# One second-product unit a turn, and Strassen's seven products for the last ten g tiles of a fused attention and feed-forward kernel

## The chip, the cores and the metric

The kernel runs on one core of a Trainium2 chip. The metric is the device time of one execution in microseconds, the median of three runs. The core has five engines with queues of their own: PE (matmuls; PEld is its weight load), DVE (vector), ACT (scalar), POOL (GpSimd) and SP, which issues most DMAs. [...]

## The reference

Cosine attention over 8 batches of 12 heads, 448 positions, 64 wide, and then a feed-forward layer with a hard swish:

```
q_n = q / (norm(q) + 1e-06);  k_n = k / (norm(k) + 1e-06)
scores = q_n @ k_n.T / tau
attn = exp(scores - max) ;  attn = attn / (sum + 1e-09)
x = (attn @ v), heads side by side         # 3584 tokens x 768
h = x @ w_in                               # 768 -> 2048
g = h * clip(h + 3, 0, 6) / 6
out = g @ w_out                            # 2048 -> 768, f32
```

## The kernel before

Heads are taken in pairs: 6 pairs a batch, 48 in all. A pair is a *turn* of the loop over `i`. The first 18 pairs run from an order written out by hand (`PLAN`); from `FIRST` = 18 on, the loop at the end of the kernel issues turn after turn, with every engine's order fixed by the program. Turn `i` issues on PE the rest of the values of pair i-1 (`VA`, L434), the scores of pair i (`SC`, L394) and a few *units* of the feed-forward layer for earlier batches, which fill PE while ACT does the exponentials (`EX`, L412). Batch b's feed-forward work lies in the turns of batch b+1 and later. After turn 47 there is no attention left, and units alone run to the end.

There are two kinds of unit, and each takes one PSUM bank from a ring of six (`bank_of(None)`). `mm1_unit(b, fc)` (L514, *first product*) multiplies 128 columns of `w_in` with the batch's x, transposed, in `xT`: six matmuls of 448 columns. ACT's relu (L523) and DVE's product (L529) turn it into a slab of `gT`. A batch has 16. `mm2_unit(b, t, m)` (L550, *second product*) multiplies a tile of 128 tokens of `gT` with a half (384 columns) of `w_out`: 16 matmuls. ACT (L561) or DVE (L563), in turns, copies the bank to an `o` tile, and SP stores it with two DMAs (L571). Two batches share a `gT` buffer of 7 tiles of 128 tokens, so that a batch with an even number has 3 tiles (6 units) and one with an odd number 4 (8 units).

`units[i]` says how many units turn i takes. Before, a batch's second-product units are spread with `n_lag`: one a turn, and two in the first and the last turn of a batch when 8 are to be placed. The first turn of a batch (i = 18, 24, 30, 36, 42) takes two first products that are left over and no new one; the new batch's first products begin in the turn after it. Each of those reads all six head pairs of the batch in `xT`. A pair's attention output reaches `xT` by a DMA transpose that SP issues: `back_two` (L498) for two pairs, `back_crossbar` (L486) for one. For the last pair of a batch it is issued in the first turn of the next, after `finish_values`, and in SP's queue behind what was queued earlier: the stores of `o`, the load of q or k (`load_qk`, L174) and, in every other turn, four loads of v (`load_v`, L186).

Other names that matter. `raws` are seven buffers of q or k as loaded (f32), `sqs` two of their squares, `vr` three of v. POOL squares (L203), normalises (`NM`, L246), casts v (L265) and copies a part of the keys (`km`, L351). DVE sums the squares (L215), copies keys (L341), finishes the values (L454, L455).

The two lines that place the second-product units of a batch:

```
n_lag = [len(lag) // 2 - 2, 1, 1, 1, 1, len(lag) // 2 - 2]
units[(b + 1) * HP + n] = carry + lag[: n_lag[n]] + u if n == 0 else carry + u + lag[: n_lag[n]]
```

After turn 47 come, in this order: two first products of batch 6, six second products of batch 6, the 16 first products of batch 7 and its 8 second products, the last one in two halves of 192 columns; one of the last half's two stores goes by ACT's queue.

Of the kernel before, what the change touches and what calls it, by code (L numbers as in the profile page):

```python
# [8 lines left out]
FP32 = mybir.dt.float32  # L9
BF16 = mybir.dt.bfloat16  # L10
AF = mybir.ActivationFunctionType
ALU = mybir.AluOpType
# [6 lines left out]
ORDER = "111111111111111111111111111111222222"  # L19
# [42 lines left out]
def kernel(  # L62
# [10 lines left out]
    nc = tc.nc  # L73
    B, H, S, D = q.shape
# [3 lines left out]
    HP = H // 2  # L78
    NP = B * HP
    CC = d_model // 128  # L80
    FCN = d_ff // 128
    MH = d_model // 2
# [8 lines left out]
    const = ctx.enter_context(tc.tile_pool(name="const", bufs=1))  # L91
# [20 lines left out]
    }  # L112
    at_n = {1: 0, 2: 0}
    NV, NR = 3, 7
    vr = [const.tile([128, 4, 5, D], FP32, name=f"vr{i}", tag=f"vr{i}") for i in range(NV)]
    NVX = 4
    vx = [const.tile([128, 8, D + 1], BF16, name=f"vx{i}", tag=f"vx{i}") for i in range(NVX)]
    raws = [const.tile([128, 2, 7, D], FP32, name=f"raw{i}", tag=f"raw{i}") for i in range(NR)]
    sqs = [const.tile([128, 2, 7, D], FP32, name=f"sq{i}", tag=f"sq{i}") for i in range(2)]
    nrms = [const.tile([128, 7, 2, D], BF16, name=f"nrm{i}", tag=f"nrm{i}") for i in range(3)]  # L120
    n2s = [const.tile([128, 2, 14], FP32, name=f"n2{i}", tag=f"n2{i}") for i in range(2)]
    rs = [
# [21 lines left out]
    def needs(*what):  # L144
        for w in what:
            assert w in issued or any(x < 0 for x in w[1:] if isinstance(x, int)), w
# [121 lines left out]
    unread = {}  # L268

    def bank_of(name, reads):  # L270

        bank = {"Y": Y, "Z": Z}[name] if name else next_bank()
        key = id(bank)
        assert not unread.get(key), name
        unread[key] = reads
        return bank, key
# [261 lines left out]

        post["a"].append(relu)

    def mm2_unit(b, t, m, end=None):
        assert not weights
        g = gT[(b // 2) % 2]
        ps, key = bank_of(None, 1)
        width = MH if end is None else MH // 2
        cols = slice(m * MH + width * (end or 0), m * MH + width * (end or 0) + width)
        for fc in range(FCN):
            c0 = (S + SR) * (b % 2) + 128 * t if t < 3 else SM
            lhs = g[:, fc, c0 : c0 + 128]
            nc.tensor.matmul(  # L550
                ps[:, 0:width],
                lhs,
                w_out_sb[:, fc, cols],
                start=(fc == 0),
                stop=(fc == FCN - 1),
            )

        def store():
            o = sb.tile([128, MH], FP32, name="o", tag="o", bufs=4)
            if on_act:  # L560
                nc.scalar.copy(out=o[:, 0:width], in_=ps[:, 0:width])  # L561
            else:
                nc.vector.tensor_copy(out=o[:, 0:width], in_=ps[:, 0:width])  # L563
            unread[key] = 0
            for e in range(2):
                if t < 3:
                    r = out[b * S : (b + 1) * S].rearrange("(p c) m -> c p m", c=7)[2 * t + e + b % 2]
                else:
                    r = out[(b - 1 + e) * S : (b + e) * S].rearrange("(p c) m -> c p m", c=7)[6 * (1 - e)]
                eng = nc.scalar if end == 1 and e else nc.sync  # L570
                eng.dma_start(out=r[:, cols], in_=o[64 * e : 64 * e + 64, 0:width])  # L571

        evac_n[0] += 1
        on_act = evac_n[0] % 2 == 1
        post["a" if on_act else "v"].append(store)

    def second(b):
        nt = 3 + b % 2
        u = [(mm2_unit, b, t, m) for t in range(nt) for m in range(2)]
        return u if b < B - 1 else u[:-1] + [u[-1] + (0,), u[-1] + (1,)]  # L580

    units = {}
    carry, lag = [], []
    for b in range(B - 1):
        first = [(mm1_unit, b, fc) for fc in range(FCN)]
        n_lag = [0, 0, 1, 1, 2, 2] if b == 1 else [1, 1, 1, 1, len(lag) // 2 - 2, len(lag) // 2 - 2]
        n_first = [1, 3, 3, 3, 2, 2] if carry else [3, 3, 2, 2, 2, 2]
        if b > 1:  # L590
            n_first = [0, 3, 3, 3, 3, 2]
            n_lag = [len(lag) // 2 - 2, 1, 1, 1, 1, len(lag) // 2 - 2]
        for n in range(HP):
            u = [first.pop(0) for _ in range(n_first[n])]
            units[(b + 1) * HP + n] = carry + lag[: n_lag[n]] + u if n == 0 else carry + u + lag[: n_lag[n]]
            carry, lag = [], lag[n_lag[n] :]
        carry, lag = first, second(b)
    units[NP] = carry + lag

    FG = d_ff // 2  # L600
    weights = [
# [51 lines left out]
    def do(op, *args):  # L653
        OPS[op](*args)
        key = (op,) + tuple(a for a in args if isinstance(a, int))
        if op not in ("RE", "NM", "LQ"):
            issued.add(key[:3] if op == "SC" else key)
# [26 lines left out]
    psum_s = startup.enter_context(tc.tile_pool(name="psum_s", bufs=1, space=bass.MemoryType.PSUM))  # L684
    SC = [psum_s.tile([128, 2, 512], FP32, name=f"SC{n}", tag=f"SC{n}") for n in range(2)]

    stream = [u for i in range(HP, NP + 1) for u in units[i]]
    stream += [(mm1_unit, B - 1, fc) for fc in range(FCN)] + second(B - 1)
    by_kind = {"1": [u for u in stream if u[0] is mm1_unit], "2": [u for u in stream if u[0] is mm2_unit]}
    first = [by_kind[x].pop(0) for x in ORDER]  # L690
    stream = first + [u for u in stream if u not in first]


    for line in PLAN:
# [3 lines left out]
    if FIRST + 6 < NP:  # L698
        do("LQ", FIRST + 6)
    for i in range(FIRST, NP):  # L700
        n_u = len(units[i])
        even = i % 2 == 0

        def prepare(*what):
            for op, n, *args in what:
                if n < (NP // 2 if op in ("NO", "LV") else NP):
                    do(op, n, *args)

        if i > FIRST:
            do("VA", i - 1, 3)  # L710
        for g in range(3):
            do("SC", i, g)
        for g in range(3):
            do("EX", i, g)
        for g in range(1, 4):
            if ("VA", i - 1, g) not in issued:
                do("VA", i - 1, g)
        do("FI", i - 1)

        if (i - 1) % HP > 3:  # L720
            do("XB", i - 1)
        elif even:
            do("XP", i - 2)
        if even:
            prepare(("XD", i + 2))
        do("UU", 1)
        do("SC", i, 3)
        do("EX", i, 3)
        if not even:
            prepare(("CS", i + 1))  # L730
        prepare(("SQ", i + 5, "p", 0, 7))
        n = 2
        do("UU", n - 1)
        if not even:
            prepare(("CK", i + 1), ("CK", i + 2))
        if not even:
            prepare(("NO", (i + 3) // 2))
        do("UU", n_u - n)
        prepare(("NM", i + 3, "p"), ("VC", i + 2, "p"), ("RE", i + 5))
        if even:  # L740
            prepare(("XD", i + 3))
        prepare(("LQ", i + 7))
        if not even:
            prepare(("LV", (i + 5) // 2))
        do("VA", i, 0)
# [2 lines left out]
    do("VA", NP - 1, 2)  # L748
    do("FI", NP - 1)
    do("XB", NP - 1)  # L750
    do("UU", len(units[NP]))
    do("UU", len(stream))


# [33 lines left out]
```

## Time and profile before

| | us |
|---|---|
| median of three runs | 418.32 (418.11 to 419.28) |
| the profiled execution | 418.05 |
| its span, first to last instruction | 415.9 |
| last attention matmul ends, PE | about 355.2 |
| PE's last matmul gives up its slot | about 412.0 |
| first-product unit, 6 matmuls x 448 | 1.135 |
| second-product unit, 16 matmuls x 384 | 2.60 |
| a turn with three first products and one second | 7.82 |
| a turn with two first products and one second | 6.69 |
| mean granted TensorE clock | 1.000 |

The chain in order of time shows, for each stretch of PE, when it begins and how long it lasts; successive entries without a gap mean that PE had work all the time. Matmuls are pipelined: a unit's record ends about 0.16 us after it has given up PE to the next one. In a timeline row the first figure is the start and the second the time from the first instruction's start to the last one's end; what stands in brackets is how long the engine had been idle and what ended it. "DMA to landing" is the time from a DMA's issue until its data are there.

The DMA's issues, with the median time from issue to landing: 448 KB of q or k 4.1 to 4.3 us, 128 KB of v 4.0, a store of 96 KB 2.2, a transpose into `xT` 3.9.

### The profile page before, as it was taken

What the parts mean: (1) busy time and instruction counts of PE and PEld (TensorE: products, weight loads), DVE (VectorE), ACT (ScalarE), POOL (GpSimd) and SP (SyncE); (2) the same over time, 40 slices, a digit from 0 to 9 for tenths busy, and PEclk for the clock granted to TensorE, in tenths of its full rate; (3) what the DMA queues carried; (4) which work ended last, traced back from release to release, by engine and by line L of the source; (5) the groups of instructions that cost most, each with busy time, mean ns of one, the idle gap of its engine ahead of it and who ended that gap; (6) DMA issues with size and microseconds to landing.
All of it is one profiled execution on the core that took longest, in us unless ns stands there. A gap on an engine that the chain in (4) does not pass through costs nothing.

```text
span 415.9 us, 9613 instructions
## 1 busy us (share of the span) xinstructions
PE 409.2 (98%) x3792; PEld 242.4 (58%) x3792; DVE 217.0 (52%) x419; ACT 268.0 (64%) x591; POOL 183.1 (44%) x190
## 2 busy tenths in 40 slices
PE   7999999999999999999999999999999999999996
PEld 4666556556665555555555556555555555655564
DVE  6898778856236545465445554565454443315410
ACT  6899998887547755857756765766766774105400
POOL 7798755464236356365465365374373200000000
PEclk9999999999999999999999999999999999999999
DMA  8999999789787866777976858777975421330033
GB/s 294 293 229 264 194 284 230 142 128 260 146 206 158 195 161 153 170 188 136 196 183 132 198 138 180 184 159 147 181 174 71 97 58 38 65 77 20 2 76 76
DMA packets 91564, 65.31 MB, mean 157 GB/s; under 512 B 56064, under 2 KB 89984, under 8 KB 91520
## 3 DMA queue, kind: packets, MB, share of 16 engines
q1 hardware_dynamic: 87728, 58.37, 61.1%
q0 software_dynamic: 3712, 6.29, 9.0%
q8 instruction: 29, 0.48, 0.5%
q14 instruction: 15, 0.12, 0.1%
q10 hardware_dynamic: 80, 0.05, 0.0%
HBM read 47.19 MB, written 11.01 MB: 140 GB/s over the span
## 4 chain that ended last, share of the span: by engine, by line
PE 98%; DVE 1%; issue 0%; ACT 0%; ACTq 0%
PE M L514 24%; PE M L550 23%; PE PV L434 12%; PE Z L550 7%; PE Y L514 6%; PE Y L550 6%; PE M L394 6%; PE Z L514 5%; PE PV L621 3%; PE Z L394 1%; PE Y L394 1%; PE SC L394 1%; PE Z L291 1%; PE Y L616 1%; PE SC L391 0%; DVE on L455 0%
## 5 line engine op out<-in xcount | busy, mean ns | idle before, releaser
L550 PEld LDWEIGHTS <-gT 128*128 128x128 bf16 x912 | 88.6, 98 | 58.4
L412 ACT ACTIVATE at<-M 128x448 bf16<-128x448 f32 x198 | 98.6, 565 | 33.2 <-PE M L394 21.0
L514 PE MATMUL M<-xT,w_in_sb 128*128 128x448 bf16 x528 | 110.7, 352 | 0.0
L514 PEld LDWEIGHTS <-w_in_sb 128*128 128x128 bf16 x768 | 71.6, 98 | 62.9 <-issue 2.5
L550 PE MATMUL M<-w_out_sb,gT 128*128 128x384 bf16 (+1 forms) x592 | 99.3, 324 | 0.0
L246 POOL TENSOR_TENSOR nrm<-raw,r 128x896 bf16<-128x896 f32 (+1 forms) x48 | 77.8, 1625 | 32.9 <-ACT r L234 25.2
L529 DVE SCALAR_TENSOR_TENSOR gT<-u,M 128x448 bf16<-128x448 bf16 x88 | 54.6, 620 | 54.3 <-ACT u L523 54.0
L434 PEld LDWEIGHTS <-at 128*128 128x128 bf16 (+1 forms) x1536 | 54.8, 97 | 24.6 <-issue 15.4
L203 POOL TENSOR_TENSOR sq<-raw 128x896 f32<-128x896 f32 (+3 forms) x39 | 63.4, 1628 | 10.4 <-DMA raw<-in_k_dram 5.0
L523 ACT ACTIVATE u<-M,bias 128x448 bf16<-128x448 f32 x88 | 58.1, 661 | 14.4 <-PE M L514 14.3
L434 PE MATMUL PV<-vx,at 128*128 128x65 bf16 (+1 forms) x1536 | 64.3, 194 | 0.2 <-DVE on L455 0.2
L351 POOL COPY km<-tT 64x128 bf16<-64x128 bf16 x34 | 9.8, 290 | 103.6 <-PE M L394 54.8
L215 DVE TENSOR_REDUCE n<-sq 128x14 f32<-128x896 f32 (+1 forms) x50 | 51.8, 1041 | 3.8 <-ACT sq L201 3.6
L412 ACT ACTIVATE at<-Z 128x448 bf16<-128x448 f32 x49 | 27.6, 564 | 12.9 <-PE M L394 12.7
L561 ACT COPY o<-M 128x384 f32<-128x384 f32 (+1 forms) x19 | 8.9, 471 | 39.8 <-PE M L550 39.7
L563 DVE COPY o<-M 128x384 f32<-128x384 f32 x18 | 10.0, 558 | 46.2 <-PE M L550 34.5
L455 DVE TENSOR_TENSOR on<-PV,rc 128x512 bf16<-128x512 f32 x48 | 33.2, 691 | 1.7
L394 PE MATMUL M<-tT,kz 64*128 64x448 bf16 (+1 forms) x175 | 31.3, 351 | 0.0
L550 PE MATMUL Z<-w_out_sb,gT 128*128 128x384 bf16 (+1 forms) x176 | 29.1, 319 | 0.0
L265 POOL CAST vx<-vr 128x512 bf16<-128x512 f32 x44 | 27.2, 622 | 2.9 <-DMA vr<-in_v_dram 1.6
L412 ACT ACTIVATE at<-Y 128x448 bf16<-128x448 f32 x47 | 26.6, 567 | 2.2 <-PE Z L394 2.2
L514 PE MATMUL Y<-xT,w_in_sb 128*128 128x448 bf16 x126 | 27.3, 353 | 0.0
(78 smaller groups left out, 335.3 us busy)
## 6 DMA issues: line engine op xcount, KB each, us to landing
vr<-in_v_dram SPq DMA_DIRECT2D x96, 128.0 KB, 4.0
raw<-in_k_dram SPq DMA_DIRECT2D x24, 448.0 KB, 4.3
raw<-in_q_dram SPq DMA_DIRECT2D x24, 448.0 KB, 4.1
out_dram<-o SPq DMA_DIRECT2D x110, 96.0 KB, 2.2
w_in_sb<-in_moe_w_in_dram POOLq DMA_DIRECT2D x4, 768.0 KB, 10.4
w_out_sb<-in_moe_w_out_dram POOLq DMA_DIRECT2D x4, 768.0 KB, 8.6
tT<-nrm SPq DMA_TRANSPOSE x34, 3.3
xT<-on SPq DMA_TRANSPOSE x25, 3.9
```

The lines of the kernel that those rows point to most:

```text
L203: engines[e].tensor_tensor(out=o, in0=i, in1=i, op=ALU.mult)
L215: nc.vector.tensor_reduce(out=n2s[d % 2][:, j % 2, c], in_=sq[:, :, :, :].rearrange("p g c d -> p (g c) d")[:, c, :], axis=AX.X, op=ALU.add,)
L246: engines[e].tensor_tensor(out=nrm[:, :, g, :].rearrange("p c g d -> p g c d"), in0=raw_of[j][:, g, :, :], in1=rs[d % 2][3][:, j % 2, :] . ...
L265: (engines[e].copy if e == "a" else engines[e].tensor_copy)(out=o, in_=f)
L394: nc.tensor.matmul(o, ks, qt[rows], start=True, stop=True)
L412: nc.scalar.activation(out=o, in_=x, func=AF.Exp, scale=inv_tau)
L434: nc.tensor.matmul(pv_out(j, h), at[rows, n, q_cols(i // HP, j)], vt[rows, 3 + h if name == "M" else 5 * h + int(name[1]), :], start=(name ...
L455: nc.vector.tensor_tensor(out=on[:, :, :, :].rearrange("p j h d -> p h j d"), in0=pv4[:, :, :, 0:D], in1=rc[:, :, :].to_broadcast([128, 2, ...
L514: nc.tensor.matmul(ps[:, 0:S], w_in_sb[:, cc, fc * 128 : (fc + 1) * 128], x[:, cc, 0:S], start=(cc == 0), stop=(cc == CC - 1),)
L523: nc.scalar.activation(out=u[:, :], in_=ps[:, 0:S], func=AF.Relu, bias=half_bias, scale=1.0 / 6.0)
L529: nc.vector.scalar_tensor_tensor(out=g[:, fc, c0 : c0 + S], in0=u[:, :], scalar=1.0, in1=ps[:, 0:S], op0=ALU.min, op1=ALU.mult,)
L550: nc.tensor.matmul(ps[:, 0:width], lhs, w_out_sb[:, fc, cols], start=(fc == 0), stop=(fc == FCN - 1),)
```

## The change

The seven products. Two tiles of g, A, and the weights W are cut into blocks: row i of A is a tile, its columns are the even (A_i1) and the odd (A_i2) slabs of 128; W has the even and odd slabs as rows and the two halves of 384 columns as columns. A product is 8 matmuls of 384 columns. Products 1, 6 and 7 multiply a sum of blocks of A with a sum of blocks of W; 2, 5, 3 and 4 have a sum on one side only. Products 2, 5 and 6 accumulate into the bank in which 4, 3 and 1 lie, which has to be read by ACT or DVE first.

- **Turns.** Each turn from 18 to 47 takes exactly one second-product unit. All of batches 1 to 4 and the last tile of batch 5 are done there. What is left are ten tiles: three of batch 5, all of batches 6 and 7.
- **Weight sums**, once. Three sums of 8 slabs x 384 columns into new buffers, in 12 pieces of 768 columns on POOL in turns 41 to 45 (1, 2, 3, 3, 3 pieces); `y4` in place in `w_out_sb`, 4 pieces on POOL in turn 47; `y3` in place, one instruction of 3072 columns on DVE after turn 47.
- **g sums**, five for each of the five pairs, 128 x 1024 bf16 each, "2" and "5" in place in `gT`: for the first pair on POOL in turn 46, for the others on DVE after turn 47.
- **Buffers.** `raws`, `sqs` and `vr` become parts of one tile `big`; the sums and four f32 tiles of 384 columns (`wide`) lie where those buffers were, once they are no longer used.
- **The end.** 35 products in place of 14 units, mixed with the first products of batch 7. Where a product is finished, ACT copies or DVE adds (and POOL subtracts once a pair); four results a pair are stored.

The diff, cut to its core:

```diff
+    big = const.tile([128, (NR + 2) * RAW + NV * VAL], FP32, name="big", tag="big")
-    raws = [const.tile([128, 2, 7, D], FP32, name=f"raw{i}", tag=f"raw{i}") for i in range(NR)]
-    sqs = [const.tile([128, 2, 7, D], FP32, name=f"sq{i}", tag=f"sq{i}") for i in range(2)]
+    raws = [item((i + 1) % NR) for i in range(NR)]
+    sqs = [item(NR + i) for i in range(2)]
...
+    TILES = [(0, 4), (0, 5), (0, 6)] + [(1, n) for n in range(7)]
...
+    def weight_sums(what, c0, n, e="p"):
+        w = w_out_sb[:, :, :].rearrange("p (c k) m -> p c k m", k=2)[:, c0 : c0 + n]
+        b11, b12, b21, b22 = (w[:, :, k, m] for k in range(2) for m in (LEFT, RIGHT))
...
+        o, x, y, op = {
+            "1": (b11, b11, b22, ALU.add),
+            "6": (b11, b11, b12, ALU.add),
+            "7": (b21, b21, b22, ALU.add),
+            "y3": (b12, b12, b22, ALU.subtract),
+            "y4": (b21, b21, b11, ALU.subtract),
+        }[what]
...
+        engines[e].tensor_tensor(out=o, in0=x, in1=y, op=op)
...
+    def g_sum(n, what, e="v"):
+        a11, a12, a21, a22 = (block(n, i, k) for i in range(2) for k in range(2))
...
+            "6": (s["6"], a21, a11, ALU.subtract),
+            "2": (a21, a21, a22, ALU.add),
+            "7": (s["7"], a12, a22, ALU.subtract),
+            "5": (a12, a12, a11, ALU.add),
+            "1": (s["1"], a11, a22, ALU.add),
...
+    def product_unit(n, name, end=None):
...
+        base = {"2": "4", "5": "3", "6": "1"}.get(name)
+        if base is None:
+            banks[n, name] = bank_of(None, 1)
+        ps, key = banks.pop((n, base)) if base else banks[n, name]
...
+        for c in range(KC):
+            nc.tensor.matmul(m, lhs[:, c, :], rhs[:, c, c0 : c0 + width],
+                start=(base is None and c == 0), stop=(c == KC - 1), skip_group_check=True)
...
+        def finish():
+            if name == "4":
+                nc.scalar.copy(out=d, in_=m)
+            elif name == "3":
+                nc.vector.tensor_tensor(out=d, in0=m, in1=d, op=ALU.add)
+            elif name == "2":
+                copied(1, LEFT)
+            elif name == "5":
+                nc.vector.tensor_tensor(out=f, in0=d, in1=m, op=ALU.subtract)
+                post["a"].append(lambda: copied(0, RIGHT))
+                nc.gpsimd.tensor_tensor(out=d, in0=d, in1=parts[n, "2"][:, :], op=ALU.subtract)
+            elif name == "1":
+                nc.vector.tensor_tensor(out=f, in0=m, in1=f, op=ALU.add)
+            elif name == "6":
+                added(1, RIGHT, d)
+            else:
+                added(0, LEFT, f)
...
-        n_lag = [0, 0, 1, 1, 2, 2] if b == 1 else [1, 1, 1, 1, len(lag) // 2 - 2, len(lag) // 2 - 2]
-        n_first = [1, 3, 3, 3, 2, 2] if carry else [3, 3, 2, 2, 2, 2]
-        if b > 1:
-            n_first = [0, 3, 3, 3, 3, 2]
-            n_lag = [len(lag) // 2 - 2, 1, 1, 1, 1, len(lag) // 2 - 2]
...
+    lag = [u for b in range(1, B - 3) for u in second(b)] + second(B - 3)[-2:]
+    carry = firsts(1, FCN - 2, FCN - 1)
+    for b in range(2, B - 1):
+        first = firsts(b, *range(FCN))
+        for n, x in enumerate([0, 3, 3, 3, 3, 2]):
+            u = [first.pop(0) for _ in range(x)]
+            units[(b + 1) * HP + n] = carry + u + [lag.pop(0)]
+            carry = []
+        carry = first
+    pieces = [(weight_sums, x, c, 2) for x in "167" for c in range(0, KC, 2)]
+    for i, n in ((NP - 7, 1), (NP - 6, 2), (NP - 5, 3), (NP - 4, 3), (NP - 3, 3)):
+        side[i] = [pieces.pop(0) for _ in range(n)]
+    side[NP - 2] = [(g_sum, 0, x, "p") for x in "62751"]
+    side[NP - 1] = [(weight_sums, "y4", c, 2) for c in range(0, KC, 2)]
...
+    units[NP] = carry[:1] + [(weight_sums, "y3", 0, KC, "v")] + carry[1:] + products(0, "42") + sums(1, "62") + products(0, "35")
+    for n, x in enumerate("176"):
+        units[NP] += f[n : n + 1] + products(0, x) + sums(1, "751"[n])
+    for n, x in enumerate("4325176"):
+        units[NP] += f[3 + n : 4 + n] + products(1, x) + (sums(2, "62751"[n]) if n < 5 else [])
+    for n in range(10, FCN):
+        units[NP] += f[n : n + 1]
+    units[NP] += products(2, "4") + sums(3, "62") + products(2, "3") + sums(3, "75") + products(2, "25") + sums(3, "1")
+    units[NP] += products(2, "1") + sums(4, "62") + products(2, "76") + sums(4, "751") + products(3, "4325")
+    units[NP] += products(4, "43") + products(3, "1") + products(4, "25") + products(3, "76") + products(4, "16")
+    units[NP] += [(product_unit, 4, "7", x) for x in range(2)]
...
+        for f, *args in side.get(i, []):
+            f(*args)
         prepare(("LQ", i + 7))
```

## The prediction

> **What bounds the kernel now.** I read the page's busy table first, then the chain of work that ended last, then the timeline by engine where the change cuts.
>
> ```profile
> PE 409.2 (98%) x3792; PEld 242.4 (58%) x3792; DVE 217.0 (52%) x419; ACT 268.0 (64%) x591; POOL 183.1 (44%) x190
> ...
> PEclk9999999999999999999999999999999999999999
> DMA  8999999789787866777976858777975421330033
> ...
> PE 98%; DVE 1%; issue 0%; ACT 0%; ACTq 0%
> PE M L514 24%; PE M L550 23%; PE PV L434 12%; PE Z L550 7%; PE Y L514 6%; PE Y L550 6%; PE M L394 6%; PE Z L514 5%; PE PV L621 3%; PE Z L394 1%; PE Y L394 1%; PE SC L394 1%; PE Z L291 1%; PE Y L616 1%; PE SC L391 0%; DVE on L455 0%
> ```
>
> A busy PE need not be at its peak, but the chain in order of time shows PE without a gap: a second-product unit (L550) takes 2.60 us for 16 matmuls, 162.5 ns each, a first-product unit (L514) 1.135 us. So PE work removed comes off the end, and any wait put into PE's queue is added to it. The DMA row is close to full until the last loads; that is the neighbour to watch.
>
> **What is removed.** Ten tiles of g cost 20 units of 16 matmuls, 320; five pairs with seven products of 8 cost 280. 40 x 162.5 ns = **6.5 us less PE**. The half-width split of the last unit stays in kind (2 x 1.33 us before, 2 x 0.66 after) and cancels. Six units move from the turns to the end (14 of the 20 were there before), which costs PE nothing, but the turns lose 15.6 us of cover over the same loads.
>
> **Added at the end: waits of PE on its own banks.** Products 2, 5 and 6 accumulate into the bank of 4, 3 and 1 once that has been read. In three places of the order the two stand side by side, or the reader is late: 4 then 2 and 3 then 5 of the first pair, 1 then 6 of the last. The rows for such a read:
>
> ```profile
> 406.78 2.76 PE L550 MATMUL Y<-w_out_sb,gT 128*128 128x384 bf16 x16
> 406.98 0.56 DVE L563 COPY o<-M 128x384 f32<-128x384 f32 x1 [4.64 <-PE M L550]
> 409.62 0.48 ACT L561 COPY o<-Y 128x384 f32<-128x384 f32 x1 [4.72 <-PE Y L550]
> ```
>
> The DVE copy begins 0.20 us after the unit before it gave up PE, and takes 0.56; ACT's takes 0.48. With 0.05 for the way back (an estimate: 0.03 us lie between ACT's end and DVE's start at 374.99) a wait is 0.73 on ACT and 0.81 on DVE: 0.73 + 2 x 0.81 = **2.35 us**. Bounds: 1.5 if the way out were hidden, 3 if a g sum stands ahead of each.
>
> **DVE's new sums.** 20 sums of 128x1024 and one of 128x3072, all bf16; no row has two bf16 inputs. From above, the f32 square on DVE: 1083 ns for 896, so 1.24 us for 1024 and 3.7 for 3072. From below, the same dtypes as copies: 448 columns f32 to bf16 cost 622 ns and bf16 to bf16 382, so 0.54 ns an element less; 1083 / 896 - 0.54 = 0.67 ns, or 0.69 and 2.1 us. I take the lower, dtype and place being what the copies differ by. Then DVE keeps up: interleaved with first products, a step lasts 1.135 + 1.30 = 2.43 us and holds a gT product (0.62), a sum (0.69) and an add (0.56). After the last first product come ten sums in a row with adds between; I lined them up, and the fifth pair's last sum ends 11.9 us after that point, the add of the fourth pair's product 3 at 12.5, half a microsecond before product 5 wants it at 13.0. At the upper price that add is 2.7 us late, and earlier ones 2.2, 0.7 and 1.0: 6.6 us in all.
>
> [...]
>
> **GpSimd's new sums.** 12 weight pieces and y4's 4 of 768 columns, five g sums of 1024. Rows: nrm and sq of 896 follow each other at 1.63 us (258.59, 260.22, 261.86), so 1.40 and 1.86 us. An odd turn's nrm starts 6.2 us after the turn does (130.50 against 124.32). From there in turn 43: nrm, cast, 3 pieces; nrm, cast, 3; km, cast, 3; five sums; y4: 27.5 us of new work, ending 8.1 us into the last turn. Product 4, the first reader, starts about 10.0 in, and its last piece is needed at 11.0. Slack 2.9 us, so nothing is charged. Bounds: one input at the cast's price (620 ns for 512) would be faster still; nrm's 448-column row (938 ns) makes the 27.5 into 31.6, 1.2 us too late.
>
> [...]
>
> **Where the shorter turns hit.** The new batch's first unit needs the transposed attention of the last head pair, sent by SP behind the loads and stores queued ahead of it. Turn 18:
>
> ```profile
> 117.99 1.30 PE L514 MATMUL Y<-xT,w_in_sb 128*128 128x448 bf16 x6
> 119.12 2.76 PE L550 MATMUL Z<-w_out_sb,gT 128*128 128x384 bf16 x16
> 121.54 0.59 SPq L174 DMA_DIRECT2D raw<-in_k_dram  x1
> 121.72 2.76 PE L550 MATMUL M<-w_out_sb,gT 128*128 128x384 bf16 x16
> 122.23 1.21 SPq L486 DMA_TRANSPOSE xT<-on  x1
> 125.95 1.30 PE L514 MATMUL M<-xT,w_in_sb 128*128 128x448 bf16 x6
> ```
>
> The transpose lands 3.8 us after its issue, at 126.03. Its reader, the sixth matmul of the unit at 125.95, runs at 126.90. The change takes the second L550 unit out of this turn, so the reader comes at 124.30, while SP's queue up to the transpose is the same: **1.75 us** of PE wait. Lowest landing of this transpose in the trace is 2.4 us (0.35 wait), highest 5.4 (3.3). Behind the waiting matmul stands the whole of PE; ACT's relu and DVE's product come after it.
>
> The same place in turns 24, 30, 36 and 42: landings 173.75, 218.67, 268.13, 314.21; readers now 174.20, 221.48, 268.78, 316.07. Two of these turns (30, 42) held a second unit, so their readers come 2.60 earlier, 218.88 and 313.47. Margins 0.45, 0.21, 0.65 and -0.74. Landings there spread from 3.3 to 5.3 us, so I take **0.9 us**; 0 if all land in 3.3, 4.8 if all take 5.3.
>
> **The very end.** The last two half units are half as long, so the stores bunch up on SP. Rows:
>
> ```profile
> 404.93 8.24 SPq L571 DMA_DIRECT2D out_dram<-o  x9
> 410.70 1.48 PE L550 MATMUL M<-w_out_sb,gT 128*128 128x192 bf16 x16
> 412.26 0.32 ACT L561 COPY o<-M 128x192 f32<-128x192 f32 x1 [2.16 <-PE M L550]
> ```
>
> SP's last store ends at 413.17, 1.14 us after PE (slot end 412.03). After the change product 6 gives two stores 0.8 us past its end, then the halves two and one: five at 0.59 us, the last ending 3.75 past product 6, or 2.4 past PE's end 1.33 us later: **1.25 us** more; 0.6 if SP is not the last to be done.
>
> **Sum.** -6.5 + 2.35 + 0 + 0 + 1.75 + 0.9 + 1.25 = -0.25 us. The profiled execution took 418.05 us (span 415.9 and 2.15 around it), so 417.8; the median of the runs shown is 0.27 above that execution, which makes **418.1, as good as no change**. A measurement of this kernel can tell 0.3%, 1.25 us, from no change. The sum's own range, without the rivals, is 416.5 to 419.8.
>
> **Rivals.**
> Faster, the transposes arrive in time: the loads behind which they queue ebb with the units gone. Only the waits at the end stay: -6.5 + 2.35 + 1.25 = -2.9, **415.4**. For it: three of four margins are positive. Against: turn 18's queue is unchanged to the very transpose.
> Slower, GpSimd is late with y4: its two-input sums on distinct bf16 tensors cost a quarter more an element than nrm and sq, 6.9 us more, 4.0 past the slack, PE standing before product 4: **422.1**. It decides from 10% on (2.9 of 27.5). For it: nrm broadcasts one input and sq reads one tensor twice. Against: 448 to 896 columns cost 1.67 ns an element for f32 inputs, twice as many bytes.
> Slower, DVE's sums run at the f32 price: +6.6, **424.7**. For it: no such row exists. Against: the bf16 copies.
> The edit not doing what it says: raw, square and v buffers become one tile; a wait tracked by the tile instead of the region would bind loads to sums in every turn. In the two kernels' instruction lists the turns carry the same waits, so I give this little.
>
> **Chances.** Sum as worked 0.42, faster rival 0.28, GpSimd 0.17, DVE 0.08, other 0.05. Faster than 0.3%: 0.27 of the faster rival and 0.10 of the sum's low end, 0.37. Within: 0.29 of the sum and 0.04 of the rivals' edges, 0.33. Slower: 0.30. Range 414.8 to 421.0: below lies the faster rival with cheaper bank waits, above the DVE case and the worse part of GpSimd's.
>
> **What would show it.** PE's waits: three of 0.7 to 0.8 us at the end, one of 1.75 at the first unit of turn 19, on the transpose. DVE's 128x1024 sums at 0.69 against 1.24; GpSimd's 128x768 at 1.40 against 1.75. SP's last store ending 2.4 us after PE. Wrong above all if PE shows no wait at turn 19, or a wait on GpSimd before product 4.

## The result, and the profile after

The changed kernel takes 421.14 us, the median of five runs (420.58 to 421.97), the kernel before in the same rounds 418.11: a ratio of 1.0070, interval 1.0049 to 1.0092. It is slower by 3 us, and 0.14 us above the top of the predicted range. The profiled execution took 420.71 us with a span of 418.9, where before it was 418.05 and 415.9. The two spans are compared in what follows.

The page of the changed kernel: the busy row, the clock granted to PE, and the chain that ended last by engine.

```profile
PE 404.5 (97%) x3744; PEld 238.1 (57%) x3744; DVE 240.3 (57%) x456; ACT 270.2 (65%) x595; POOL 226.3 (54%) x216
...
PEclk9999999999999999999999999999999998999998
...
PE 81%; POOL 10%; DMA 3%; ACT 2%; DVE 1%; issue 1%; SPq 1%; POOLq 0%; ACTq 0%; DVEq 0%
```

PE is busy 4.7 us less than before, although 6.5 us of matmuls went: some of what is left ran slower. One slice of the clock row, the 34th, is no longer full (the last one lies after most of PE's work). And GpSimd, which was not in the chain at all, holds 10% of it. The view of waits of PE says what it stood for (total, times, longest):

```profile
PE M L684 <- POOL w_out_sb L637: 2.4, 1, 2.4
PE M L525 <- DMA xT<-on: 1.7, 1, 1.7
PE M L684 <- DVE big L715: 0.7, 1, 0.7
PE Y L684 <- DVE big L723: 0.6, 1, 0.6
PE M L684 <- ACT big L713: 0.6, 1, 0.6
```

Four of these five were forecast, in place and nearly in size. The first was the rival with GpSimd. (A wait here is 0.16 us shorter than PE's loss, because the record of the unit before ends that much after it has given up PE. In the sums below the loss is taken.)

The timeline of that stretch, right after turn 47:

```profile
339.24 7.97 POOL L637 TENSOR_TENSOR w_out_sb<-w_out_sb 128x768 bf16<-128x768 bf16 x4
...
343.69 1.14 PE L684 MATMUL M<-w_out_sb,gT 128*128 128x384 bf16 x6
...
343.96 1.75 DVE L637 TENSOR_TENSOR w_out_sb<-w_out_sb 128x3072 bf16<-128x3072 bf16 x1
345.63 0.61 DVE L540 SCALAR_TENSOR_TENSOR gT<-u,Z 128x448 bf16<-128x448 bf16 x1
346.16 1.59 DVE L661 TENSOR_TENSOR big<-gT,gT 128x1024 bf16<-128x1024 bf16 x1
347.26 0.48 PE L684 MATMUL M<-w_out_sb,gT 128*128 128x384 bf16 x2 [2.43 <-POOL w_out_sb L637]
...
348.36 4.07 PE L684 MATMUL M<-w_out_sb,gT 128*128 128x384 bf16 x16 [0.61 <-ACT big L713]
...
353.14 1.14 PE L684 MATMUL M<-w_out_sb,gT 128*128 128x384 bf16 x6 [0.72 <-DVE big L715]
```

Product 4 begins at 343.69, does six of its eight matmuls, and stands from 344.67 to 347.26 for the last piece of `y4`. Then 16 matmuls (products 2 and 3) take 4.07 us where 16 took 2.76 before. The windows over half a microsecond each give the reason in the column after the five engines, the granted clock:

```profile
346.00:346.50 0.50, 0.00 (x0) 0.00 (x0) 0.50 (x2) 0.00 (x0) 0.50 (x1) 1.00 0.00 0
...
347.70:348.20 0.50, 0.04 (x1) 0.00 (x0) 0.47 (x2) 0.38 (x1) 0.00 (x0) 0.50 0.00 0
...
350.50:351.00 0.50, 0.50 (x3) 0.28 (x2) 0.00 (x0) 0.00 (x0) 0.00 (x0) 0.50 0.00 0
351.00:351.50 0.50, 0.50 (x5) 0.27 (x4) 0.00 (x0) 0.39 (x1) 0.00 (x0) 0.96 0.00 0
```

The clock is still full while PE stands, falls to half some 3 us after it fell idle, when it is working again, and is full again from 351.0. That costs another 1.31 us.

GpSimd's own rows, with the mean duration of one in ns before the last bar, and the four pieces of `y4` by shortest, median and longest (a tile's view):

```profile
L637 POOL TENSOR_TENSOR big<-w_out_sb 128x768 bf16<-128x768 bf16 x12 | 19.3, 1635 | 0.0
...
L661 POOL TENSOR_TENSOR big<-gT 128x1024 bf16<-128x1024 bf16 x3 | 6.4, 2121 | 0.0
```

```profile
L637 POOL TENSOR_TENSOR w_out_sb<-w_out_sb x4: 1632/1636/3192, 339.2 to 344.0; 128x768 bf16<-128x768 bf16 x4
```

Pieces of 768 follow each other at 1.60 us and sums of 1024 at 2.09, where 1.40 and 1.86 had been worked out. And the last piece of `y4`, from 344.01 to 347.20, takes twice as long as the others, while DVE does `y3` and then a g sum, which itself takes 1.59 in place of the 0.69 that the others of its kind take.

The two other places. Turn 19's first unit (PE, then SP's queue in front of the transpose):

```profile
123.04 1.11 PE L525 MATMUL M<-xT,w_in_sb 128*128 128x448 bf16 x5
125.83 0.35 PE L525 MATMUL M<-xT,w_in_sb 128*128 128x448 bf16 x1 [1.68 <-DMA xT<-on]
```

```profile
117.89 3.19 SPq L559 DMA_DIRECT2D out_dram<-o  x4
121.12 0.58 SPq L185 DMA_DIRECT2D big<-in_k_dram  x1
121.81 1.21 SPq L497 DMA_TRANSPOSE xT<-on  x1
```

And the end, five stores in a row on SP's queue, from 413.25 to 416.44, when PE has given up its last slot at 413.72:

```profile
413.25 3.19 SPq L559 DMA_DIRECT2D out_dram<-o  x5
```

The accounts from one span to the other, in us: PE work -6.5; turns 18 to 47 +2.19; `y4` +2.59; half clock +1.31; three bank waits +2.44 (a bank is one of the kernel's tiles of 128 x 512 f32 in PSUM, which its matmuls write); after PE's last slot +1.31 (5.18 against 3.87); before turn 18 -0.32. Together +3.0, the difference of the spans.

### The profile page after: what moved, and what is told of

Read it like the earlier page. It is cut to its first block, busy times and chain, and to the rows that moved or that the text cites. A ratio compares the mean times of both kernels' runs of the same rounds, so it can differ in the third digit from the quotient of the medians.

```text
span 418.9 us, 9604 instructions
## 1 busy us (share of the span) xinstructions
PE 404.5 (97%) x3744; PEld 238.1 (57%) x3744; DVE 240.3 (57%) x456; ACT 270.2 (65%) x595; POOL 226.3 (54%) x216
## 4 chain that ended last, share of the span: by engine, by line
PE 81%; POOL 10%; DMA 3%; ACT 2%; DVE 1%; issue 1%; SPq 1%; POOLq 0%; ACTq 0%; DVEq 0%
PE M L525 21%; PE M L571 12%; PE PV L445 10%; PE M L684 8%; PE Y L525 5%; PE M L405 5%; PE Z L525 4%; PE Z L571 4%; POOL big L637 3%; PE Y L571 2%; PE Y L684 2%; POOL w_out_sb L637 2%; DMA xT<-on 2%; POOL big L661 1%; PE PV L792 1%; ACT at L423 1%
## 5 line engine op out<-in xcount | busy, mean ns | idle before, releaser
L257 POOL TENSOR_TENSOR nrm<-big,r 128x896 bf16<-128x896 f32 (+1 forms) x48 | 77.7, 1624 | 30.2 <-ACT r L245 23.0
L571 PEld LDWEIGHTS <-gT 128*128 128x128 bf16 x576 | 56.2, 98 | 38.5
L214 POOL TENSOR_TENSOR big<-big 128x896 f32<-128x896 f32 (+3 forms) x39 | 63.4, 1628 | 11.9 <-DVE gT L540 4.6
L571 PE MATMUL M<-w_out_sb,gT 128*128 128x384 bf16 x384 | 66.2, 326 | 0.0
L226 DVE TENSOR_REDUCE n<-big 128x14 f32<-128x896 f32 (+1 forms) x50 | 51.8, 1040 | 3.8 <-ACT big L212 3.6
L721 POOL TENSOR_TENSOR big<-big,o 128x384 f32<-128x384 f32 x5 | 5.6, 1125 | 55.5 <-DVE big L719 55.5
L465 DVE RECIPROCAL rc<-PV 128x8 f32<-128x8 f32 x48 | 9.9, 206 | 37.6 <-PE PV L445 35.9
L525 PE MATMUL Y<-xT,w_in_sb 128*128 128x448 bf16 x138 | 30.0, 352 | 0.1
L276 POOL CAST vx<-big 128x512 bf16<-128x512 f32 x44 | 27.2, 622 | 1.6 <-DMA big<-in_v_dram 1.5
L684 PEld LDWEIGHTS <-gT 128*128 128x128 bf16 x160 | 16.0, 100 | 15.8 <-issue 5.8
```

The costliest lines, as they stand in the source:

```text
L214: engines[e].tensor_tensor(out=o, in0=i, in1=i, op=ALU.mult)
L226: nc.vector.tensor_reduce(out=n2s[d % 2][:, j % 2, c], in_=sq[:, :, :, :].rearrange("p g c d -> p (g c) d")[:, c, :], axis=AX.X, op=ALU.add,)
L257: engines[e].tensor_tensor(out=nrm[:, :, g, :].rearrange("p c g d -> p g c d"), in0=raw_of[j][:, g, :, :], in1=rs[d % 2][3][:, j % 2, :] . ...
L525: nc.tensor.matmul(ps[:, 0:S], w_in_sb[:, cc, fc * 128 : (fc + 1) * 128], x[:, cc, 0:S], start=(cc == 0), stop=(cc == CC - 1),)
L571: nc.tensor.matmul(ps[:, 0:MH], g[:, fc, c0 : c0 + 128], w_out_sb[:, fc, cols], start=(fc == 0), stop=(fc == FCN - 1),)
L684: nc.tensor.matmul(m, lhs[:, c, :], rhs[:, c, c0 : c0 + width], start=(base is None and c == 0), stop=(c == KC - 1), skip_group_check=True,)
```

## The experiments

Each run is read in three stretches of its profiled execution: *turns*, from turn 18's first unit to the first unit after turn 47 (before, less 15.6 us for the six units that lay there, 222.88); *end*, from there to where PE gives up its last slot (65.93 would be without any wait: 18 first products of 1.135 and 35 products of 1.30); *tail*, from there to the end of the span.

| kernel | median, us (range, runs) | ratio to before, interval | turns | end | tail |
|---|---|---|---|---|---|
| changed | 421.14 (420.58 to 421.97, 5) | 1.0070, 1.0049 to 1.0092 | 225.07 | 72.30 | 5.18 |
| e1_y4_on_dve | 418.72 (416.31 to 420.87, 12) | 1.0008, 0.9988 to 1.0029 | 225.41 | 68.41 | 5.15 |
| e2_filler | 421.52 (419.20 to 424.13, 10) | 1.0078, 1.0054 to 1.0102 | 224.59 | 71.02 | 5.18 |
| e3_second_first | 424.73 (423.49 to 426.50, 5) | 1.0157, 1.0132 to 1.0181 | 226.30 | 74.11 | 5.21 |
| e4_turns_only | 420.03 (419.55 to 421.70, 6) | 1.0050, 1.0030 to 1.0070 | 224.69 | other work | 3.9 |
| e5_order | 419.17 (417.27 to 421.41, 12) | 1.0016, 0.9990 to 1.0041 | 227.11 | 70.02 | 5.17 |
| e6_stores | 421.22 (418.79 to 424.15, 11) | 1.0056, 1.0027 to 1.0086 | 226.51 | 72.56 | 4.16 |
| e7_end_mended | 414.95 (413.91 to 419.89, 12) | 0.9931, 0.9903 to 0.9959 | 225.06 | 66.92 | 4.16 |
| e8_sp_too | 412.70 (412.20 to 414.25, 6) | 0.9860, 0.9827 to 0.9892 | 222.88 | 66.92 | 4.13 |
| e9_sp_only | 419.38 (417.50 to 422.33, 12) | 1.0024, 1.0000 to 1.0049 | 223.23 | 72.29 | 5.15 |
| e10_y3_halves | 412.05 (411.60 to 414.58, 6) | 0.9853, 0.9826 to 0.9881 | 222.88 | 66.36 | 4.1 |
| e11_two_pieces_dve | 418.00 (416.43 to 421.63, 12) | 1.0004, 0.9981 to 1.0027 | 224.45 | 68.41 | 5.15 |

The executions of the kernels that mend one part scatter by several us. The stretches show two places: the turns lost between 1.6 and 4.2 us against 222.88 in kernels with the same units and the same queue of SP there, and what lies ahead of turn 18, the same work in every kernel, took from 116.3 to 119.3 us (119.3 in the profiled executions of e7_end_mended and e10_y3_halves, which are 2.4 and 2.5 us above their medians). So one part is judged by its stretch, and the median by the kernels that mend all.

**y4 on the other engine.** The four pieces on GpSimd become one sum of 3072 on DVE:

```diff
-    side[NP - 1] = [(weight_sums, "y4", c, 2) for c in range(0, KC, 2)]
+    side[NP - 1] = [(weight_sums, "y4", 0, KC, "v")]
```

> y4 is one sum of 3072 columns on DVE in turn 47, where DVE has gaps, in place of four pieces on GpSimd; nothing else differs from the changed kernel. If GpSimd's lateness is what holds product 4 (2.6 us wait) and that wait is what halves the clock (about 1.4 us in products 2 and 3), both go: 421.1 becomes about 417.2, the granted clock is 1.000, and PE's first wait after turn 47 is the bank wait of product 2. Rival: the wait only moves, to y3 or a g sum in DVE's queue, which is now 1.8 us longer: 419.5 to 421.

The end took 68.41 in place of 72.30, 3.89 less; the wait on GpSimd is gone, the clock is full throughout, and the other waits are as they were. DVE's g sum beside it took 0.69 again. That is the wait and the half clock together, as the theory had it. The median came down less, to 418.72 and not to 417.2; in the profiled execution (418.64) what lies ahead of turn 18 took 1.2 us and the turns 0.34 us longer than in the changed kernel's.

**The clock apart from the wait.** 15 matmuls whose result is overwritten stand in front of product 4, so that PE works while `y4` is made:

```diff
+        if (n, name) == (0, "4"):
+            for _ in range(15):
+                nc.tensor.matmul(m, lhs[:, 0, :], w_out_sb[:, 1, RIGHT], start=True, stop=True, skip_group_check=True)
```

> 15 extra matmuls of 384 columns (2.4 us) stand before product 4 and are overwritten by it; y4 stays late on GpSimd. If PE's idle time is what halves the clock, the wait is filled, the clock stays at 1.000 and products 2 and 3 run at full rate: 1.3 to 1.4 us less than the changed kernel, 419.8, though PE does 2.4 us more work. Rival: the clock falls for another reason (the bank waits behind, or power): no gain, 421 to 423, and the half-rate stretch is still there or elsewhere.

The timeline of PE and a window of that run:

```profile
343.17 2.60 PE L685 MATMUL M<-w_out_sb,gT 128*128 128x384 bf16 x15
345.61 1.64 PE L687 MATMUL M<-w_out_sb,gT 128*128 128x384 bf16 x8
347.85 2.76 PE L687 MATMUL M<-w_out_sb,gT 128*128 128x384 bf16 x16 [0.61 <-ACT big L716]
```

```profile
348.00:349.00 1.00, 1.00 (x8) 0.59 (x7) 0.00 (x0) 0.00 (x0) 0.00 (x0) 1.00 0.00 0
```

The 16 matmuls behind product 4 take 2.76 us at full clock, where they took 4.07, and the end is 1.28 us shorter, although `y4` comes no sooner. The half clock is a cost of its own, and here the idle PE is its cause. The median did not fall with it (421.52); a gain of this size is lost in the scatter of the turns, so this is shown by the stretch alone.

**The queue in front of y4.** This run separates how long GpSimd's queue is from what happens to its last piece. The last two of the twelve weight pieces go to DVE, `y4` stays:

```diff
     side[i] = [pieces.pop(0) for _ in range(n)]
+    side[NP - 3][1:] = [(*p, "v") for p in side[NP - 3][1:]]
```

> The changed kernel with the last two of the twelve weight pieces, at the end of turn 45, on DVE in place of GpSimd; y4 stays on GpSimd. Theory (y4 is late because GpSimd's queue before it is 5.4 us longer than worked out, piece by piece): GpSimd begins y4 3.2 us sooner, its last piece ends before DVE begins y3 and so takes 1.6 us in place of 3.2, PE does not wait for it, and the clock stays full: 3.9 us less from the first unit after turn 47 to PE's last, 68.4 in place of 72.3 us there, the other waits as they were; some 417.2 us if the turns take 225.1 as in the changed kernel's profiled run. Rival (y4 is late because GpSimd and DVE share the way to SBUF, whatever the queue): the last piece is still some 3 us, PE waits 0.8 us or more for it, and about 70 us stand there.

The view of the tile and the timeline (GpSimd, DVE):

```profile
L637 POOL TENSOR_TENSOR w_out_sb<-w_out_sb x4: 1631/1637/1641, 335.9 to 340.7; 128x768 bf16<-128x768 bf16 x4
```

```profile
343.28 1.75 DVE L637 TENSOR_TENSOR w_out_sb<-w_out_sb 128x3072 bf16<-128x3072 bf16 x1
...
345.48 0.69 DVE L661 TENSOR_TENSOR big<-gT,gT 128x1024 bf16<-128x1024 bf16 x1
```

All four pieces take 1.63 us now, DVE's g sum is back at 0.69, PE does not wait for `y4`, and the end takes 68.41, just as with `y4` on DVE. So the doubled piece and the slow g sum belong to their meeting in time, and `y4` had been late by less than two pieces. The rival (still late by 0.8 us or more) falls. The median, 418.00, is 0.8 above the 417.2 expected.

**The turns alone.** All that the change adds at the end is taken out again: no sums, no seven products; the ten tiles are 20 ordinary units after turn 47.

```diff
...
-    pieces = [(weight_sums, x, c, 2) for x in "167" for c in range(0, KC, 2)]
...
-    units[NP] += [(product_unit, 4, "7", x) for x in range(2)]
+    last = second(B - 1)
+    units[NP] = carry + second(B - 3)[:-2] + second(B - 2) + firsts(B - 1, *range(FCN)) + last[:-1]
+    units[NP] += [last[-1] + (x,) for x in range(2)]
```

> The first half of the change alone: one second-product unit a turn, and the ten tiles left are done by ordinary units at the end, without products or sums. PE has the work of the kernel before, so the time is that kernel's plus what the turns lose, 2.1 us: 420.2, with a wait of 1.7 us at the first unit of turn 19. Rival: the turns lose nothing by themselves, and what the changed kernel loses there comes from GpSimd's and DVE's sums: 418.1.

It is slower than the kernel before by 1.9 us in the median. The stretch from turn 18 to 47 lost 1.81 us (224.69 against 222.88), 1.52 of it in turn 19 and 0.26 in turn 25; after turn 47 it took 72.48, which is the 56.88 of before and the 15.6 of the six units moved, to 0.01. The placement costs this much by itself.

**Another order of units.** In the turn that waits for the transpose, the second product goes ahead of the first products:

```diff
-            units[(b + 1) * HP + n] = carry + u + [lag.pop(0)]
+            units[(b + 1) * HP + n] = [lag.pop(0)] + u if n == 1 else carry + u + [lag.pop(0)]
```

> In the second turn of each batch (19, 25, 31, 37, 43) the second-product unit is issued before the three first products, which gives the transposes 2.6 us more; all else is the changed kernel. If PE waits there for the last transpose because the turn before lost its second unit, all of the 2.1 us in the turns goes: about 419.0, no wait of PE on a DMA. Rival: DMAs as a whole are the bound of the shorter turns: the wait comes back at another place, 420.5 or more.

The wait on the DMA is gone, and the turns took longer still, 226.30. The view of waits names what came in its place:

```profile
PE M L684 <- POOL w_out_sb L637: 2.9, 2, 2.6
...
PE M L405 <- DVE gT L540: 1.0, 3, 0.3
...
PE Y L405 <- DVE gT L540: 0.7, 2, 0.3
```

The scores of the next turn need banks which DVE has not read yet; turns 20, 26, 32, 38 and 44 are each 0.7 us longer than 7.82, 3.5 in all. At the end this kernel had 6.8 us at half clock, after two gaps, and so its end took 74.11. Neither the theory nor the rival had this, and as a repair it was a miss. It gave three more instances of GpSimd and DVE in each other's way, which the part on the hardware uses.

**SP's order.** The transposes go ahead of the loads which stand in front of them:

```diff
-    if FIRST + 6 < NP:
-        do("LQ", FIRST + 6)
...
+        if i == FIRST:
+            do("LQ", FIRST + 6)
+        elif i % HP == 0:
+            prepare(("LV", (i + 4) // 2))
...
-        if not even:
+        if not even and (i + 1) % HP:
             prepare(("LV", (i + 5) // 2))
```

> The changed kernel with SP's order alone edited: in the first turn of each batch the transposes of the last head pairs are queued ahead of the load of q or k (turn 18) and of the four loads of v (turns 24, 30, 36, 42), which otherwise stand in front of them. Theory (the turns' loss is the place of the transposes in SP's queue): PE's waits on a DMA at the first product of turns 19, 25, 31, 37 and 43, 1.7 us and some tenths in the profiled run of the changed kernel, are gone; from turn 18 to the first unit after turn 47 it takes 222.9 us in place of 225.1; the end is as before with its wait on GpSimd and its half clock; 421.1 - 2.2 = 418.9 us, with less spread between executions than the changed kernel's parts had so far. Rival (the loss is the cover that PE lost over the same loads, so a transpose that comes earlier makes a load come later): waits on loads of q, k or v appear in the turns, and the time stays at 421.

The turns took 223.23, 1.84 less; what is left of the wait is 0.19 (0.35 of PE's time), in turn 19:

```profile
PE M L684 <- POOL w_out_sb L637: 2.4, 1, 2.4
...
PE M L525 <- DMA xT<-on: 0.2, 1, 0.2
```

No wait for q, k or v takes its place, so the rival falls. The end is as in the changed kernel, to 0.01. Two things were missed. The median is 419.38, 0.5 above what was expected. And the executions scatter as before; their mean clocks lie between 0.990 and 0.997, and as only one was profiled, what made the others differ stays open. The kernel before ranged from 417.58 to 421.00 in the same rounds.

**Bank waits.** Product 2 of the first pair goes behind 3, and product 1 of the last one unit earlier:

```diff
-    units[NP] = carry[:1] + [(weight_sums, "y3", 0, KC, "v")] + carry[1:] + products(0, "42") + sums(1, "62") + products(0, "35")
+    units[NP] = carry[:1] + [(weight_sums, "y3", 0, KC, "v")] + carry[1:] + products(0, "432") + sums(1, "62") + products(0, "5")
...
-    units[NP] += products(4, "43") + products(3, "1") + products(4, "25") + products(3, "76") + products(4, "16")
+    units[NP] += products(4, "43") + products(3, "1") + products(4, "251") + products(3, "76") + products(4, "6")
```

> Only the order of products changes: 4, 3, 2, 5 in the first pair in place of 4, 2, 3, 5, and product 1 of the last pair stands before 7 and 6 of the pair before it. If the bank waits cost what they show in the changed kernel (0.76, 0.87 and 0.81 us), all three go and PE's only wait behind turn 47 is the one for y4: 421.1 - 2.4, and 0.4 back because PE now works through all of the half-clock stretch: 419.1. Rival: the waits move to other products, since DVE has the same adds to do: 420.5 to 421.

All three bank waits are gone from the list, and the end is 2.28 us shorter. In the same execution turn 19 was 3.85 us longer than 7.82, so that its span, 419.0, is no shorter than the changed kernel's; the median, 419.17, shows the gain. The windows of that turn say why it was so long (the granted clock is the column after the five engines):

```profile
126.00:127.00 1.00, 0.50 (x3) 0.29 (x3) 0.00 (x0) 0.12 (x1) 0.00 (x0) 1.00 1.21 228
127.00:128.00 1.00, 1.00 (x6) 0.50 (x4) 0.45 (x1) 0.95 (x2) 0.58 (x2) 0.70 0.74 165
128.00:129.00 1.00, 1.00 (x5) 0.34 (x3) 0.17 (x1) 0.16 (x1) 0.93 (x1) 0.50 0.91 204
...
130.00:131.00 1.00, 1.00 (x5) 0.41 (x4) 0.65 (x3) 0.42 (x2) 0.41 (x1) 0.59 0.91 332
```

PE stood 2.0 us for the transpose by the waits, and ran at half clock from 127.4 to 130.8, which is 1.7 of the 3.85. So half clock came behind the wait in turn 19 too.

**The last stores.** One of the two stores of each of the last three results goes by ACT's queue:

```diff
-            result(*rows[i], cols, o, end)
+            result(*rows[i], cols, o, 1 if n == 4 and name in "67" else None)
```

> For products 6 and 7 of the last pair one store of two goes by ACT's queue, otherwise the changed kernel. If SP, issuing five stores one after the other, sets the end, the time from PE's last slot to the end of the span falls from 5.2 us to about 4.0: 421.1 - 1.25 = 419.9. Rival: the last landing sets it, not the issue: no change, 421.1.

The tail took 4.16 in place of 5.18, 1.02 less. Turn 19 cost 3.18 in that execution, all of it the wait, at full clock (3.02 by the waits); the median, 421.22, shows nothing of the gain.

**All of them.** First the three edits at the end together (`y4` on DVE, order, stores), then SP's order as well:

> y4 on DVE, the other order of products and the stores on two queues, together. If the losses add up, 421.1 - 3.9 - 2.4 - 1.25 = 413.5, 4.5 us under the kernel before; the clock stays at 1.000, and what is left of the 6.5 us are the 2 us in the turns. Rival: they overlap, and DVE's queue becomes the bound of the last stretch: 415.5 or more.

> The kernel of e7_end_mended, and in SP's queue the transpose of a batch's last pair goes before the four loads of v (turns 24, 30, 36, 42) and before the load of q or k (turn 18). If the wait in the turns is one of SP's order, the transposes are issued 2.7 us earlier in four turns and 0.7 in turn 18: of 2.1 us about 1.1 go, 412.4. Rival: the DMAs are the bound, and the v loads, now later, make the casts of v and the values wait: as e7_end_mended or slower.

The three at the end bring that stretch to 66.92, 5.38 less, and the tail to 4.16; the turns still lose 2.18, and the median is 414.95. That lies between the sum, 413.5, and the rival, 415.5: of the 7.55 us in the sum 6.40 came, and most of the rest is a new wait, 0.97 us of PE, that the next view shows. With SP's order the median is 412.70 us, a ratio to before of 0.9860: the turns took 222.88, the figure of before to the hundredth, where half of the loss had been expected to stay, and the executions lie within 2.1 us. One wait was left at the end:

```profile
PE M L684 <- DVE w_out_sb L637: 0.8, 1, 0.8
```

Product 3 waits for `y3`, now that nothing ahead of it does. Splitting that sum into two halves:

```diff
-    units[NP] = carry[:1] + [(weight_sums, "y3", 0, KC, "v")] + carry[1:] + products(0, "432") + sums(1, "62") + products(0, "5")
+    units[NP] = carry[:1] + [(weight_sums, "y3", c, KC // 2, "v") for c in (0, KC // 2)] + carry[1:] + products(0, "432") + sums(1, "62") + products(0, "5")
```

> The kernel with all four edits (y4 on DVE, product 2 behind 3, the last stores on two queues, SP's order), in which y3 is summed in two instructions of 1536 columns in place of one of 3072, so that product 3 can begin on the first half while the second is made. Theory (the only wait that is left at the end, 0.8 us for y3, is a wait for the whole instruction): the first half is there 0.88 us sooner, product 3 waits under 0.1 us, and 0.8 us come off: 412.7 - 0.8 = 411.9. Rival (the next thing in line, ACT's read of product 4 or the bank of product 3, takes over at once): 412.5 to 412.7.

The wait is gone from the list; the four products after the first two units are one row without an idle stretch:

```profile
344.41 5.77 PE L684 MATMUL M<-w_out_sb,gT 128*128 128x384 bf16 x32
```

32 matmuls need 5.36 us (32 x 162.5 ns and 0.16), so some 0.4 is still lost in small gaps. The end is 0.56 us shorter and the median, 412.05, 0.65 lower, of which 0.23 is also in the kernel before as it ran beside each (417.87 against 418.10); the two intervals overlap, so that of the two kernels this one is ahead by its stretch, not by its ratio. Both are faster than the kernel before and the changed one.

## Why the prediction was wrong

**What failed: GpSimd's sums, "Slack 2.9 us, so nothing is charged".** The place was right: from the start of turn 47 (333.66) product 4 began 10.03 us in, as worked out. But `y4` ended 13.54 us in, not 8.1. The 5.4 us between are accounted for. Nine weight pieces from turn 43 on, at 1.60 in place of 1.40, make 1.8; five g sums, at 2.09 in place of 1.86, 1.15; three pieces of `y4` 0.6; the last piece, at 3.19 in place of 1.40, 1.8. The sum is 5.35; less the slack of 2.9 it is 2.45, and PE stood 2.59. Two errors lie in it. The price was taken from rows whose two inputs are not two bf16 tensors (nrm broadcasts one, sq reads one twice), and the new pieces cost 2.1 ns an element (1.60 us for 768) where those rows cost 1.8 (1.63 for 896). Whether the two tensors, their type or the blocks in which they are read make them dearer was not tested. The right price stood in the prediction as its upper bound, nrm's row of 448 columns: by it the 27.5 us of new work are 31.6, and by the measured spacings 31.25. And the sums on GpSimd and DVE were priced one by one, though they would run side by side. By the price alone, all four pieces of `y4` at 1.60, PE would have waited some 0.85 us (3.75 less 2.9). The meeting with DVE added the other 1.6, the last piece's 3.19 less 1.60.

The rival with GpSimd, forecast at 422.1, had these sums a quarter dearer than nrm and sq and a wait of 4.0 us. The quarter was the author's assumption, which no row of the kernel before shows; the runs gave 14% for the pieces (1.60 against 1.40), 12% for the g sums (2.09 against 1.86), and a wait of 2.59.

**What had no term: the half clock**, 1.31 us. The rival with GpSimd counted how long PE would stand, but not what a stand of that length does to the matmuls after it. The filler run shows that it is a consequence of the stand: with PE at work there, the 16 matmuls behind product 4 took 2.76 us in place of 4.07.

These two make 3.9 us; the two kernels that only bring `y4` in time are shorter by just that at the end. Without it the changed kernel's span would be 415.0, 0.65 under the 415.65 that the sum gave (415.9 less 0.25). Term by term:

- **Bank waits**: 2.35 forecast, 2.44 measured (0.76, 0.87, 0.81). Right, and the order run takes them away.
- **Turn 19**: 1.75 forecast, 1.84 in the profiled execution. The mechanism is right, and the SP run shows it. That the size came out so near is luck: over the kernels with this queue and order of units the wait was 1.2 to 3.2 us, inside the bounds given for it (0.35 to 3.3), and turn 19 lost up to 3.9 where half clock came behind the wait, which no term had.
- **Turns 25, 31, 37, 43**: 0.9 forecast; turn 25 cost 0.26, turn 37 0.12, the others nothing.
- **The end of the span**: 1.25 forecast, 1.31 measured; SP's last store ended 2.72 us after PE where 2.4 was forecast, and the store run gets 1.02 us of the loss back.
- **DVE's sums**: 0.69 us for 1024 forecast, 0.68 to 0.69 measured where GpSimd was not in the way. Its rival at the f32 price falls. So does the one in which the edit doesn't do what it says, as in the kernel with all four edits the turns take what they took before.
- **Before turn 18**: -0.32, not forecast; the change does nothing there.

The DMA row, read as close to full until the last loads, stands between 5 and 9 tenths from its eighth slice to its 31st; the SP run shows that the order in the queue, and not a full DMA, made PE wait.

The faster rival (the transposes arrive in time) is refuted by turn 19. That SP's order makes it true is what the last kernels live on.

## What to carry to other kernels

An engine that was off the critical path and is given work becomes a supplier with a due time. Price its queue up to that time by rows with the same operands, look at what its neighbour sums in just that window (a piece of 1.63 us on GpSimd took 3.19 beside DVE's sums), and treat a slack of a tenth of the work as none (2.9 of 27.5 us were not enough here). Where the expected stall is a few microseconds of PE, allow for matmuls at half clock behind it (1.31 us behind a stand of 2.59). When units are moved away from a stretch, look for the DMA that they covered, and move it forward in its queue before trying another order of units.

## What the runs showed of the hardware

**Where sums on GpSimd and DVE met, they took turns.** The slow instructions, sums on DVE with two inputs in SBUF and sums on GpSimd, fit a simple account: in each meeting the one that was issued second ended as if it had begun when the first was done, to 0.15 us. In the changed kernel GpSimd's last piece, issued at 344.01, waits for `y3` (until 345.71) and needs its own 1.6: 347.3, measured 347.20. DVE's g sum, issued at 346.16, waits until 347.20 and takes 0.69: 347.9, measured 347.75. In the kernel with the second product first, `y3` is issued 0.75 us before the third piece ends and takes 2.40 in place of 1.75, which is the rest of that piece and its own 1.75 less 0.10:

```profile
345.12 2.40 DVE L637 TENSOR_TENSOR w_out_sb<-w_out_sb 128x3072 bf16<-128x3072 bf16 x1
347.44 0.61 DVE L540 SCALAR_TENSOR_TENSOR gT<-u,Z 128x448 bf16<-128x448 bf16 x1
347.97 1.59 DVE L661 TENSOR_TENSOR big<-gT,gT 128x1024 bf16<-128x1024 bf16 x1
```

The row between them has one input in PSUM and keeps its 0.61 us. The account holds in smaller meetings too: GpSimd's subtraction once a pair takes 1.00 us alone and 1.31 where it is issued during a g sum on DVE, and the g sum issued behind it 0.79 in place of 0.69. Why the second waits, no run shows.

**A stand of PE can halve the clock, and its length alone doesn't say when.** The stand of 2.6 us before product 4 was followed by 3.4 us at half clock in each of the four profiles that have it in this form; the fall came 2.2 to 4.7 us after PE fell idle, once only when it had been back at work for 2 us. In the kernel with the second product first, with stands of 0.3 and 2.6 us close together, it lasted 6.8. In turn 19 a stand of 2.2 brought it in one execution and none in another (the kernel with `y4` on DVE, mean clock 1.000), and one of 3.2 didn't bring it.

The traces show what goes with the difference. Where a trace has several changes of the clock, they lie whole steps of 3.413 us apart (in the order run at 127.40, 130.81, 349.27 and 352.68, the third 65 steps after the first; in the changed kernel at 347.62, 351.04 and 415.89, the third 19 steps after the second), and their place in the kernel's work differs from profile to profile, as the 2.2 to 4.7 us show. The windows of single steps, PE's busy time first and the clock after the five engines, are for the stand before product 4 in the changed kernel, turn 19 in the order run, and turn 19 in the store run, where the stand of 3.2 us lies across one of the points:

```profile
344.21:347.62 3.41, 0.98 (x6) 0.46 (x5) 3.41 (x3) 0.32 (x1) 3.00 (x1) 1.00 0.07 13
...
123.99:127.40 3.41, 1.41 (x8) 0.64 (x7) 0.53 (x1) 1.86 (x5) 0.04 (x1) 1.00 1.08 259
...
122.24:125.65 3.41, 2.03 (x27) 1.04 (x24) 0.90 (x2) 2.73 (x6) 0.00 (x0) 1.00 0.81 179
125.65:129.07 3.42, 1.79 (x10) 0.96 (x10) 0.62 (x1) 1.15 (x3) 0.78 (x3) 1.00 1.16 239
```

Behind the first two the next step is at half clock, behind the last two it is full: half clock followed 0.98 and 1.41 us of busy PE in a step, and not 2.03 and 1.79 (busy as the profile models it). The last steps with work agree: 1.41 us in the changed kernel's, from 412.48, with half clock behind it, and 1.56 in the one of the kernel before, from 410.62, with full clock behind it. So what went with half clock in these steps was how much of a stand fell into one of them. No run was made to test this.
